# Batch 1's attention beside the first product, in eight and six units instead of ten and seven

## The chip, the cores and the metric

The kernel runs on one core of one Trainium2 chip. The time is device microseconds of one execution, as a median over several runs. A profiled execution shows every engine's instructions: PE (TensorE: matmuls, with the weight loads as PEld), DVE (VectorE), ACT (ScalarE), POOL (GpSimd) and SP (SyncE). PE's results go to PSUM, from where DVE or ACT bring them out.

## What is computed

Attention without a softmax for 8 batches, 12 heads, 448 positions and 64 columns a head, followed by one feed-forward layer with a residual:

```python
scores = scale * np.matmul(q, k.transpose(0, 1, 3, 2))
attn = np.maximum(scores, 0.0) ** 2 / S
attn_out = np.matmul(attn, v)
x = attn_out.transpose(0, 2, 1, 3).reshape(B, S, H * D)      # 768 columns
xn = (x - mean(x)) / np.sqrt(var(x) + 1e-06) * g_ln
out = x + np.maximum(xn @ w_ch1, 0.0) @ w_ch2                # 3072 columns between
```

The kernel takes and multiplies in bf16 and accumulates in fp32.

## The kernel before

**Tiles and stages.** A batch has three groups of four heads (`G = 3`; group n is batch n // 3). Its 448 positions are seven slots of 64 (`J = 7`). Attention is made per group: `scores` takes one or two slots of keys against a block of query positions, four 64x64 matmuls at a time in the four quarters of PE's array, into one PSUM tile `sc_ps`; ACT applies relu and writes `attn_sb` (L376), DVE squares it in place (L354, L380). `values` multiplies seven slots of a group with v in 28 such matmuls into a PSUM tile `av_ps`; DVE scales that into `xT_sb` (L403) and writes two more scaled chunks into `x_room` (`scaled`, L420). `centre` subtracts the mean over columns: ones times xT on PE, then six DVE operations.

The first product, `ffn1` (L672 on), takes one column of 128 of the 3072: six matmuls into a PSUM tile `h_ps`, then relu into `hT_sb`, by DVE (L690) or ACT (L692). `ffn1_head` (L708) does the first three columns in one go.

**The blocks.** Batches 0 and 1 are cut into two blocks of positions each, `BLK = (((0, 3), (3, 4)), ((0, 4), (4, 3)))` as (first slot, number of slots), so that the attention of one block runs beside `ffn1` of the block before. The order of the work is written out by hand; nothing reorders it, and every engine runs its part in the code's order. Two stretches matter here:

- The first: `ffn1` of batch 0's second block (256 positions a column), with four columns left over from its first block, beside the attention of batch 1's first block, which is 256 positions (41 to 66 us in the profile).
- The second: `ffn1` of batch 1's first block (256 positions) beside the attention of batch 1's second block, 192 positions (66 to 87 us).

`interleave` deals side units evenly among the main ones (`free` main units at the end are kept without any, `ahead` side units go first). The main units are the columns of `ffn1`; the side units come from `attention_block`: per group `unit(n, 0)` (slots 0 to 3, two score tiles) and `unit(n, 1)` (slots 4, 5 and 6, two score tiles, then the value product of the group before), in the first block with `transposed(n + 1)` between the two, then `last` (the last value product) and `centre`. In these two batches `transposed` has PE transpose q and k of a group into two PSUM tiles, which DVE copies out (L253); from batch 2 on (`by_dma`) it issues three transposing DMAs on SP instead, L312, L317 and L318.

**PSUM.** The pool `ps_sc` has three tiles of two banks (`[P, 2, 512]` fp32), which `scores`, `values`, `transposed`, `centre` and part of `ffn1_head` take in turn; `ps_mm` has two tiles of one bank, which the columns of `ffn1` take in turn.

**Who empties h_ps.** `since` counts columns since the last score visit: `scores` sets it to 0 and `values` to 9, `ffn1` adds one. While it is at most `turns`, DVE takes the column, else ACT. The squares of a block of batch 0 or 1 are not issued with their scores, but kept in `later` until `squares_now`, which every unit calls first, and `ffn1` at `since >= turns`:

```python
        since[0] += 1
        turns = 2 if (b, blk) == FIRST else 1
        if since[0] <= turns:
            nc.vector.tensor_scalar_max(hT[pair][:, ni, o:o + w], ps[:, :w], 0.0)
        else:
            nc.scalar.activation(hT[pair][:, ni, o:o + w], ps[:, :w], ACTF.Relu)
        if since[0] >= turns:
            squares_now()
```

After the two stretches come `ffn1` of batch 1's last block (87 to 99 us), the attention of batches 2 and 3 beside the second product of batches 0 and 1, and so on to the end. POOL's queue issues the loads: `load(n + 3, "v")` stands behind each value product of the second block and waits until that product has let go of its buffer.

Of the kernel before, what the change touches and what calls it, by code (L numbers as in the profile page):

```python
# [28 lines left out]
def kernel(  # L29
# [22 lines left out]
    nc = tc.nc  # L52
    P = 128
    HP = 64
    bf16 = mybir.dt.bfloat16
    fp32 = mybir.dt.float32
# [5 lines left out]
    J = S // HP  # L62
# [3 lines left out]
    K1 = d_model // P  # L66
    K2 = d_ff // P
    S2 = 2 * S
# [3 lines left out]
    score_scale = 1.0 / (D * S)  # L72
# [10 lines left out]
    xpool = ctx.enter_context(tc.tile_pool(name="x", bufs=1))  # L83
# [18 lines left out]
    x_room = wpool.tile([P, 2, K1, S + 2], bf16, tag="x_room", name="x_room")  # L102
# [44 lines left out]
    def load(n, names):  # L147
        if n >= len(groups):
            return
        b, m = groups[n]  # L150
        for name in names:
            if b == 1 and name != "v":
                o = (2 * m + "qk".index(name)) * 2 * S
                t = hold[:, o:o + 2 * S].rearrange("p (r s) -> p r s", r=2)
            elif name == "q":
                t = qbuf[m][:, D:D + 2 * S].rearrange("p (r s) -> p r s", r=2)
            else:
                t = slot(name, n)
            nc.gpsimd.dma_start(t, srcs[name][b][:, m:NP:G, :])  # L159
            qkv[name, b, m] = t  # L160
# [169 lines left out]

    FULL = (0, J)
    FIRST, LAST = (0, BLK[0][0]), (1, BLK[1][1])
    n_early = [0]

    def busy(n):
# [6 lines left out]
    def of(blk, b=0):  # L342
        o = b % 2 * S
        return slice(o + blk[0] * HP, o + sum(blk) * HP)
# [3 lines left out]
    def squares_now(n=None, but=0):  # L348

        if n is None or n in [k for k, _ in later]:
            for _, a in later[:len(later) - but]:
                nc.vector.tensor_mul(a, a, a)  # L354
            del later[:len(later) - but]

    def scores(n, slots, blk, act=False):
        g, w = st[groups[n]], blk[1] * HP
        ps = ps_sc.tile([P, 2, 512], fp32, tag="sc", name="sc_ps")
        for o, i in enumerate(slots):  # L360
            for r in range(2):
                rows = slice(r * HP, (r + 1) * HP)
                for hh in range(2):
                    cols = slice(hh * HP, (hh + 1) * HP)
                    nc.tensor.matmul(  # L365
                        ps[cols, r, o * w:(o + 1) * w], g["k"](i)[rows, cols],
                        g["q"](i, r)[rows, blk[0]:sum(blk), cols], start=True, stop=True)
        if groups[n][0]:
            a = apool.tile([P, 2, 512], bf16, tag="attn", name="attn_sb")
        else:  # L370
            o = n_early[0] % 12 * 1024
            a = early[:, o:o + 1024].rearrange("p (r s) -> p r s", r=2)
            n_early[0] += 1
        since[0] = 0
        a = a[:, :, :len(slots) * w]
        nc.scalar.activation(a, ps[:, :, :len(slots) * w], ACTF.Relu)  # L376
        if act:
            nc.scalar.activation(a, a, ACTF.Square)  # L378
        elif blk == FULL:
            nc.vector.tensor_mul(a, a, a)  # L380
        else:
            later.append((n, a))
        for o, i in enumerate(slots):
            g["attn"].append(a[:, :, o * w:(o + 1) * w])

    def values(n, blk):
        squares_now(n)
        b, m = groups[n]
        v_sb, g, w = qkv["v", b, m], st[groups[n]], blk[1] * HP
        ps = ps_sc.tile([P, 2, 512], fp32, tag="sc", name="av_ps")  # L390
        for j in range(J):
            for hh in range(2):
                rows = slice(hh * HP, (hh + 1) * HP)
                for pr in range(2):
                    cols = slice(pr * HP, (pr + 1) * HP)
                    i, r = g["where"](pr, j)
                    nc.tensor.matmul(  # L397
                        ps[cols, hh, :w], v_sb[rows, pr, j * D:(j + 1) * D],
                        g["attn"][i][rows, r, :], start=(j == 0), stop=(j == J - 1))
        if b // 2 not in xT:  # L400
            xT[b // 2] = xpool.tile([P, K1, S2], bf16, tag="xT", name="xT_sb")
        x = xT[b // 2][:, 2 * m:2 * m + 2, of(blk, b)]
        nc.vector.tensor_scalar_mul(x, ps[:, :, :w], score_scale)  # L403
        g["attn"] = []
        since[0] = 9
        if blk == FULL:
            return
        if b not in xc:
            xc[b] = x_room[:, b]
        if (b, blk) != FIRST:  # L410
            scaled(b, m, blk)

    def scaled(b, m, blk):

        for c in range(2 * m, 2 * m + 2):
            x, y = xT[b // 2][:, c, of(blk, b)], xc[b][:, c, of(blk)]
            if (b, blk) == FIRST:
                nc.scalar.mul(y, x, g_sb[:, c:c + 1])
            else:
                nc.vector.tensor_scalar_mul(y, x, g_sb[:, c:c + 1])  # L420

    def centre(b, blk):
        w = blk[1] * HP
        straight = (b, blk) == FIRST
        if straight:
            ps = ps_mm.tile([P, 512], fp32, tag="mm", name="sum_ps")[:, :w]
        else:
            ps = ps_sc.tile([P, 2, 512], fp32, tag="sc", name="sum_ps")[:, 0, :w]
        for c in range(K1):
            nc.tensor.matmul(  # L430
                ps, ones, xT[b // 2][:, c, of(blk, b)], start=(c == 0), stop=(c == K1 - 1))
        total = ps
        if not straight:
            total = room0[:, :7].rearrange("p c n -> p (c n)").bitcast(fp32)[:, :w]
            nc.scalar.copy(total, ps)
        for c in range(K1):
            nc.vector.scalar_tensor_tensor(
                xc[b][:, c, of(blk)], total, g_mean[:, c:c + 1], xc[b][:, c, of(blk)],
                op0=ALU.mult, op1=ALU.add)
# [63 lines left out]
    def transposed(n):  # L503

        if groups[n][0] < by_dma:
            transposes(*groups[n])
            return


        if by_dma * G < n < LATE:  # L510
            load(n + 2, "kq")
        keys_dma(n)
        queries_dma(n)
        if n == LATE + 1:
            put_off.append((n + 2, "kq"))
        elif n >= LATE:
            load(n + 2, "kq")

    def attention_block(b, blk):


        lo, hi, first = b * G, b * G + G, blk[0] == 0
        units = [lambda: transposed(lo)] if first else []

        def unit(n, part):
            squares_now()
            for i in range(4 * part, min(4 * part + 4, J), 2):
                scores(n, tuple(range(i, min(i + 2, J))), blk)
            if b == 1 and not first and part and n == hi - 1:
                transposed(hi)  # L530
            if part and n > lo:
                values(n - 1, blk)
                if not first:
                    load(n + 3, "v")
        for n in range(lo, hi):
            units.append(lambda n=n: unit(n, 0))
            if first and n + 1 < hi:
                units.append(lambda n=n: transposed(n + 1))
            units.append(lambda n=n: unit(n, 1))

        def last():
            values(hi - 1, blk)
            if b == 1 and not first:
                load(hi + 3, "v")
        units.append(last)
        units.append(lambda: centre(b, blk))
        return units
# [124 lines left out]
    def ffn1(b, ni, blk):  # L672


        pair, o, w = b // 2, b % 2 * S + blk[0] * HP, blk[1] * HP
        if pair not in hT:
            hT[pair] = hpool.tile([P, K2, S2], bf16, tag="hT", name="hT_sb")
        ps = ps_mm.tile([P, 512], fp32, tag="mm", name="h_ps")

        more, s = 2 if (b, blk) == LAST else 0, of(blk)  # L680
        for c in range(K1):
            nc.tensor.matmul(  # L682
                ps[:, :w + more], w1[:, c, ni * P:(ni + 1) * P], xc[b][:, c, s.start:s.stop + more],
                start=(c == 0), stop=(c == K1 - 1))
        if more:
            nc.vector.tensor_copy(fold["sums"][:, ni], ps[:, w:w + more])
        since[0] += 1
        turns = 2 if (b, blk) == FIRST else 1
        if since[0] <= turns:
            nc.vector.tensor_scalar_max(hT[pair][:, ni, o:o + w], ps[:, :w], 0.0)  # L690
        else:
# [3 lines that stand above are left out]
# [706 lines left out]
```

## Time and profile before

| | us |
|---|---|
| median of 3 runs | 514.32 |
| lowest and highest | 514.0, 515.42 |
| the profiled execution | 514.53 |
| its span, first to last instruction | 512.7 |

| busy in the span | us | share |
|---|---|---|
| PE | 504.5 | 98% |
| DVE | 387.3 | 76% |
| ACT | 309.4 | 60% |
| POOL | 129.6 | 25% |

The profile's views used here are: the chain of waits, which goes back from the last instruction to whatever released each; the busy time of each engine in a stretch; and the timeline, where instructions of one kind that follow one another stand in one row with the start of the first, the time from there to the end of the last, and their number. Matmuls are pipelined: each lasts about 0.27 us in a row while the next starts 0.11 us after it, so starts are to be compared, not ends.

### The profile page before, as it was taken

Reading aid. Unit: us, or ns where it says so; the run is one execution under the profiler, and the core shown is the slowest. Engines: PE = TensorE matmul, PEld = TensorE weight load, DVE = VectorE, ACT = ScalarE, POOL = GpSimd, SP = SyncE. Lnnn points to the kernel's source line nnn. Section 1 sums busy time; section 2 is a strip of 40 time slices with the busy share of each in tenths; the row PEclk is TensorE's granted clock in tenths of the full one; section 3 lists DMA queues with packets and bytes.
Section 4 is the critical chain, followed back from the end, with each engine's and each line's share of the span. In section 5 each row is a group of like instructions: output and inputs, shape, how many; then the busy total and the mean of one; then the engine's idle time right before and its main releaser. Section 6 shows DMA issues by size and latency. Waiting matters only on the chain.

```text
span 512.7 us, 11440 instructions
## 1 busy us (share of the span) xinstructions
PE 504.5 (98%) x4553; PEld 299.0 (58%) x4553; DVE 387.3 (76%) x745; ACT 309.4 (60%) x496; POOL 129.6 (25%) x182
## 2 busy tenths in 40 slices
PE   8899999999999999999999999999999999999996
PEld 6677788855555555555555555555555555556663
DVE  5775765389899888858789968858887968868663
ACT  5966676488678266657757266639979366630000
POOL 8335112012301266321201099501100022200000
PEclk9999999999999999999999999999999999999999
DMA  9999999999969985329995989304997393322222
GB/s 196 206 207 206 211 206 159 158 145 185 190 141 166 185 197 175 130 65 168 187 245 106 186 186 184 94 11 84 188 185 173 71 215 124 94 77 63 63 61 61
DMA packets 124486, 76.31 MB, mean 149 GB/s; under 512 B 80562, under 2 KB 120498, under 8 KB 124434
## 3 DMA queue, kind: packets, MB, share of 16 engines
q1 hardware_dynamic: 93730, 41.38, 39.6%
q0 software_dynamic: 28544, 30.91, 38.3%
q10 hardware_dynamic: 2160, 3.31, 2.8%
q8 instruction: 35, 0.57, 0.5%
q14 instruction: 17, 0.14, 0.1%
HBM read 64.69 MB, written 17.89 MB: 161 GB/s over the span
## 4 chain that ended last, share of the span: by engine, by line
PE 94%; ACT 2%; DVE 1%; DMA 1%; issue 1%; SPq 0%; DVEq 0%
PE m_ps L899 28%; PE o_ps L741 20%; PE o_ps L1109 9%; PE m_ps L1109 8%; PE h_ps L682 8%; PE sc_ps L365 8%; PE av_ps L397 6%; PE h_ps L726 2%; PE h_ps L708 2%; PE o_ps L1071 2%; ACT early L376 1%; PE tr_ps L250 1%; DMA stage_sb<-in_q_dram 1%; DMA out_dram<-o_room 1%; DVE o_room L1125 0%
## 5 line engine op out<-in xcount | busy, mean ns | idle before, releaser
L376 ACT ACTIVATE attn_sb<-sc_ps 128x896 bf16<-128x896 f32 (+4 forms) x150 | 126.3, 902 | 39.4 <-PE sc_ps L365 34.5
L903 ACT ACTIVATE hT_sb<-m_ps 128x448 bf16<-128x448 f32 x144 | 78.2, 543 | 52.0 <-PE m_ps L899 49.3
L741 PE MATMUL o_ps<-w,hT_sb 128*128 128x384 bf16 x624 | 108.3, 327 | 0.0
L741 PEld LDWEIGHTS <-hT_sb 128*128 128x128 bf16 x624 | 58.2, 98 | 45.7 <-issue 10.1
L380 DVE TENSOR_TENSOR attn_sb<-attn_sb 128x896 bf16<-128x896 bf16 x98 | 61.7, 645 | 19.8 <-ACT attn_sb L376 19.1
L682 PE MATMUL h_ps<-x_room,w 128*128 128x256 bf16 (+2 forms) x384 | 43.8, 263 | 0.4 <-ACT early L376 0.3
L1109 PEld LDWEIGHTS <-hT_sb 128*128 128x128 bf16 x312 | 29.7, 98 | 22.1 <-issue 3.0
L980 DVE TENSOR_TENSOR m_ps<-x_room,m_ps 128x448 f32<-128x448 f32 x36 | 22.6, 629 | 23.8 <-ACT hT_sb L903 23.6
L682 PEld LDWEIGHTS <-w 128*128 128x128 bf16 x384 | 33.8, 97 | 7.2 <-issue 2.8
L899 PEld LDWEIGHTS <-w 128*128 128x128 bf16 x246 | 23.9, 97 | 23.1 <-issue 0.4
L1109 PEld LDWEIGHTS <-x_room 128*128 128x128 bf16 x252 | 24.2, 98 | 17.4 <-issue 1.6
L403 DVE TENSOR_SCALAR xT_sb<-av_ps 128x896 bf16<-128x896 f32 (+2 forms) x30 | 27.0, 901 | 9.3 <-PE av_ps L397 9.2
L964 ACT COPY x_room<-m_ps 128x448 f32<-128x448 f32 x36 | 19.1, 531 | 21.6 <-PE m_ps L899 20.7
L899 PEld LDWEIGHTS <-w_sum 128*128 128x128 bf16 x210 | 20.5, 98 | 19.1
L159 POOL DMA_DIRECT2D k_sb<-in_k_dram x15 | 10.7, 712 | 81.1 <-DMA kT_sb<-k_sb 57.3
L899 PE MATMUL m_ps<-x_sum,w 128*128 128x448 bf16 x120 | 29.1, 352 | 0.1
L659 DVE BATCH_NORM_STATS2 stats<-xtok_sb 128x6 f32<-128x384 bf16 x56 | 28.3, 548 | 0.0
L159 POOL DMA_DIRECT2D v_sb<-in_v_dram x20 | 14.2, 711 | 55.5 <-PE sc_ps L365 40.7
L365 PE MATMUL sc_ps<-qT_sb,kT_sb 64*64 64x448 bf16 x392 | 28.2, 358 | 0.0
L692 ACT ACTIVATE hT_sb<-h_ps 128x256 bf16<-128x256 f32 (+1 forms) x49 | 18.0, 368 | 16.1 <-PE h_ps L682 15.2
L378 ACT ACTIVATE attn_sb<-attn_sb 128x896 bf16<-128x896 bf16 x28 | 26.6, 950 | 0.9
L397 PE MATMUL av_ps<-attn_sb,v_sb 64*64 64x448 bf16 (+2 forms) x532 | 26.2, 331 | 0.1
(196 smaller groups left out, 871.7 us busy)
## 6 DMA issues: line engine op xcount, KB each, us to landing
out_dram<-o_room SPq DMA_DIRECT2D x108, 96.0 KB, 2.8
w<-in_moe_w_ch_dram POOLq DMA_DIRECT2D x12, 384.0 KB, 14.3
w<-in_moe_w_ch_dram POOLq DMA_DIRECT2D x4, 1152.0 KB, 20.0
q_sb<-in_q_dram POOLq DMA_DIRECT2D x20, 224.0 KB, 6.2
v_sb<-in_v_dram POOLq DMA_DIRECT2D x20, 224.0 KB, 6.6
k_sb<-in_k_dram POOLq DMA_DIRECT2D x15, 224.0 KB, 6.0
kept<-room SPq DMA_DIRECT2D x4, 480.0 KB, 2.6
kept<-w_sum SPq DMA_DIRECT2D x16, 96.0 KB, 1.7
```

What stands on the lines that cost most here:

```text
L365: nc.tensor.matmul(ps[cols, r, o * w:(o + 1) * w], g["k"](i)[rows, cols], g["q"](i, r)[rows, blk[0]:sum(blk), cols], start=True, stop=True)
L376: nc.scalar.activation(a, ps[:, :, :len(slots) * w], ACTF.Relu)
L378: nc.scalar.activation(a, a, ACTF.Square)
L380: nc.vector.tensor_mul(a, a, a)
L397: nc.tensor.matmul(ps[cols, hh, :w], v_sb[rows, pr, j * D:(j + 1) * D], g["attn"][i][rows, r, :], start=(j == 0), stop=(j == J - 1))
L403: nc.vector.tensor_scalar_mul(x, ps[:, :, :w], score_scale)
L659: nc.vector.bn_stats(stats[:, n], xtok[pair][:, n * G:(n + 1) * G, t, :])
L682: nc.tensor.matmul(ps[:, :w + more], w1[:, c, ni * P:(ni + 1) * P], xc[b][:, c, s.start:s.stop + more], start=(c == 0), stop=(c == K1 - 1))
L741: nc.tensor.matmul(ps[:, :DH], hT[pair][:, ki, t * P:(t + 1) * P], w2[:, ki, cols], start=(o == 0), stop=(o == K2 - 1))
L899: nc.tensor.matmul(ps, *at, start=(first and c == 0), stop=(c == KQ - 1), skip_group_check=not first)
L903: nc.scalar.activation(hT[pair][:, n + KH * row, half * S:(half + 1) * S], ps, ACTF.Relu)
L1109: nc.tensor.matmul(ps, x[:, ki], y[ki] if isinstance(y, list) else y[:, ki], start=(first and ki == 0), stop=(ki == KH - 1), skip_group_ch ...
```

## The change

`attention_block` builds batch 1's units by hand. Units are now bundles of `two` (two slots' scores), `one` (the seventh slot's scores, and with them the value product of the group before), and `transposed`. The first block is `transposed`, then per group three `two`s and a bundle of `one`, with the next group's transposes ahead of it: eight units and `centre`. The second is six and `centre`, some with slots of two groups. Inside `one` the value product takes the columns of the `sc_ps` tile that the seventh slot leaves free, its matmuls are issued between the slot's scores and its relu, and the scaling behind that relu. `values` is split for it. Last, `turns` is 3 in the two stretches, and `since` is 0 after a shared value product, where it was 9.

```diff
+    BESIDE = [(0, BLK[0][1]), (1, BLK[1][0])]
...
-    def scores(n, slots, blk, act=False):
+    def scores(n, slots, blk, act=False, then=None):
         g, w = st[groups[n]], blk[1] * HP
         ps = ps_sc.tile([P, 2, 512], fp32, tag="sc", name="sc_ps")
...
+        end = then(ps[:, :, w:]) if then else None
         if groups[n][0]:
             a = apool.tile([P, 2, 512], bf16, tag="attn", name="attn_sb")
...
-    def values(n, blk):
+        if end:
+            end()
+            since[0] = 0
+
+    def values(n, blk, ps=None):
+        if ps is None:
+            values_of(n, blk, ps_sc.tile([P, 2, 512], fp32, tag="sc", name="av_ps"))()
+        else:
+            return values_of(n, blk, ps)
+
+    def values_of(n, blk, ps):
         squares_now(n)
...
-        ps = ps_sc.tile([P, 2, 512], fp32, tag="sc", name="av_ps")
...
+        def out_of():
...
+            nc.vector.tensor_scalar_mul(x, ps[:, :, :w], score_scale)
+            g["attn"] = []
+            since[0] = 9
...
+            if (b, blk) != FIRST:
+                scaled(b, m, blk)
+        return out_of
...
-            if b == 1 and not first and part and n == hi - 1:
-                transposed(hi)
...
+        def last():
+            values(hi - 1, blk)
+            if b == 1 and not first:
+                load(hi + 3, "v")
+
+        def two(n, i):
+            scores(n, (i, i + 1), blk)
+
+        def one(n):
+            scores(n, (J - 1,), blk, then=(lambda ps: values(n - 1, blk, ps)) if n > lo else None)
+            if n > lo and not first:
+                load(n + 3, "v")
+
+        def bundle(*parts):
+            def run():
+                squares_now()
+                for f, *at in parts:
+                    f(*at)
+            return run
+        if b == 1:
+            n = lo
+            if first:
+                units += [bundle((two, n, 0), (two, n, 2), (two, n, 4)),
+                          bundle((transposed, n + 1), (one, n)),
+                          bundle((two, n + 1, 0), (two, n + 1, 2), (two, n + 1, 4)),
+                          bundle((transposed, n + 2), (one, n + 1)),
+                          bundle((two, n + 2, 0), (two, n + 2, 2), (two, n + 2, 4)),
+                          bundle((one, n + 2))]
+            else:
+                units += [bundle((two, n, 0), (two, n, 2)),
+                          bundle((two, n, 4), (one, n), (two, n + 1, 0)),
+                          bundle((two, n + 1, 2), (two, n + 1, 4), (one, n + 1)),
+                          bundle((two, n + 2, 0), (two, n + 2, 2), (two, n + 2, 4)),
+                          bundle((transposed, hi), (one, n + 2))]
+            return units + [last, lambda: centre(b, blk)]
...
-        turns = 2 if (b, blk) == FIRST else 1
+        turns = 2 if (b, blk) == FIRST else 3 if (b, blk) in BESIDE else 1
```

More of the change, by code (lines that the diff above doesn't have):

```diff
@@ L399, in values @@
                         g["attn"][i][rows, r, :], start=(j == 0), stop=(j == J - 1))
[L400 to L411, printed above, removed]
+        def out_of():
+            if b // 2 not in xT:
+                xT[b // 2] = xpool.tile([P, K1, S2], bf16, tag="xT", name="xT_sb")
+            x = xT[b // 2][:, 2 * m:2 * m + 2, of(blk, b)]
+            nc.vector.tensor_scalar_mul(x, ps[:, :, :w], score_scale)
+            g["attn"] = []
+            since[0] = 9
+            if blk == FULL:
+                return
+            if b not in xc:
+                xc[b] = x_room[:, b]
+            if (b, blk) != FIRST:
+                scaled(b, m, blk)
+        return out_of
     def scaled(b, m, blk):
@@ L539, in attention_block @@
             units.append(lambda n=n: unit(n, 1))
[L541 to L544, printed above, removed]
         units.append(last)
```

## The prediction

> **What bounds the kernel now.** I read the page's chain of waits first, then the busy time by stretch for the two blocks that the diff touches, then the timelines of PE and DVE in them, then one row of ACT. The chain:
>
> ```profile
> PE 94%; ACT 2%; DVE 1%; DMA 1%; issue 1%; SPq 0%; DVEq 0%
> ```
>
> The end is set by PE, so a microsecond that PE loses or saves where it never waits moves the end by a microsecond. The two blocks, by stretch (length, PE, PEld, DVE, ACT, POOL busy):
>
> ```profile
> 41.00:65.80 24.80, 24.80 (x397) 19.61 (x396) 16.30 (x34) 17.25 (x33) 7.74 (x11) 1.00 1.18 209
> 66.00:87.20 21.20, 21.20 (x318) 17.14 (x318) 12.51 (x36) 15.29 (x32) 3.39 (x5) 1.00 1.24 172
> ```
>
> PE is busy all of both, and the view of waits has none of PE's from 40 to 100 us. DVE is 66% and 59% busy. PE's timeline (start, length) shows what a change of shape costs:
>
> ```profile
> 11.06 0.58 PE L250 MATMUL tr_ps<-identity,q_sb 128*64 128x128 bf16 x14
> ...
> 11.96 0.44 PE L365 MATMUL sc_ps<-early 64*64 64x192 bf16 x12
> ...
> 51.15 0.97 PE L250 MATMUL tr_ps<-identity,xtok_sb 128*64 128x128 bf16 x28
> 52.06 1.49 PE L682 MATMUL h_ps<-x_room,w 128*128 128x256 bf16 x12
> 53.47 0.52 PE L365 MATMUL sc_ps<-xtok_sb 64*64 64x256 bf16 x12
> 53.83 0.93 PE L397 MATMUL av_ps<-attn_sb,spare 64*64 64x256 bf16 x28
> 54.69 1.48 PE L682 MATMUL h_ps<-x_room,w 128*128 128x256 bf16 x12
> 56.10 0.63 PE L365 MATMUL sc_ps<-xtok_sb 64*64 64x256 bf16 x16
> 56.67 1.48 PE L682 MATMUL h_ps<-x_room,w 128*128 128x256 bf16 x12
> ```
>
> Unbroken, 18 such h_ps matmuls (63.98 us, 2.13 long, 0.27 one) start 0.109 apart; I call six a column. Four 64*64 score matmuls run at once, 0.109 a set. From 52.06 to 53.47 are 1.41 us, 12 steps and 0.09 more; from 56.10 to 56.67 are 0.57, four sets and 0.13 more. So a visit to the scores costs 0.22 us of changes. A transposes' visit costs the same: 0.09 in, and 28 steps of 0.028 and 0.12 out.
>
> DVE's timeline, first of the first block, then of the second:
>
> ```profile
> 50.61 0.42 DVE L690 TENSOR_SCALAR hT_sb<-h_ps 128x256 bf16<-128x256 f32 x1 [0.62 <-PE h_ps L682]
> 50.95 1.36 DVE L354 TENSOR_TENSOR attn_sb<-attn_sb 128x1024 bf16<-128x1024 bf16 x2
> 52.22 1.15 DVE L253 COPY xtok_sb<-tr_ps 128x896 bf16<-128x896 bf16 x2
> 54.81 0.69 DVE L403 TENSOR_SCALAR xT_sb<-av_ps 128x512 bf16<-128x512 f32 x1 [1.44 <-PE av_ps L397]
> 55.54 0.48 DVE L420 TENSOR_SCALAR x_room<-xT_sb,g_sb 128x256 bf16<-128x256 bf16 x2
> 55.93 1.02 DVE L354 TENSOR_TENSOR attn_sb<-attn_sb 128x1024 bf16<-128x1024 bf16 x2
> ...
> 75.96 0.56 DVE L403 TENSOR_SCALAR xT_sb<-av_ps 128x384 bf16<-128x384 f32 x1 [0.94 <-PE av_ps L397]
> 76.55 0.45 DVE L420 TENSOR_SCALAR x_room<-xT_sb,g_sb 128x192 bf16<-128x192 bf16 x2
> 76.92 0.82 DVE L354 TENSOR_TENSOR attn_sb<-attn_sb 128x768 bf16<-128x768 bf16 x2
> ```
>
> DVE starts things in the code's order. From start to start an eviction takes 0.34 (0.42 until it has ended), a pair of wide squares 1.27, so three 1.91, two transposes' copies 1.15, a product's scaling with its two followers 1.12. In the second block they are 0.5 a square of 768 (mean 551 ns, overlapping), 0.28 one of 384, 0.96 the scaling.
>
> **The change, part by part.** *Fewer visits.* In the first block two transposes' visits go in with the score visit behind them. From 11.06 to 11.96 transposes hand over to scores in 0.90, as they do to h_ps in 0.91, so each join saves 0.09 in and about 0.01: 0.2 for two. In the second block one score visit fewer saves 0.22 us. Together 0.42 us on the path. Matmul and weight load counts stay.
>
> *The shared tile.* It saves one of three ps_sc turns a group, worth nothing now, as PE waits for none. It adds an order: the slot's relu comes after the 28 value matmuls in the code, the scaling after that relu. How the program treats two engines in one bank is seen where columns of one h_ps tile are read by DVE (L712) and others by ACT:
>
> ```profile
> 89.05 0.33 ACT L715 ACTIVATE hT_sb<-h_ps 128x192 bf16<-128x192 f32 x1 [1.14 <-DVE x_room L712]
> ```
>
> ACT waited although its columns are others. So I let relu wait for the product, scaling for relu. The Trainium skill (PSUM — Partial Sum Buffer, "PSUM bank collisions raise a hardware error") asks that engines be kept apart by bank and not by address; a reader who took the free columns for free to use at once would by that rule be wrong. With the wait a 256-wide relu (605 ns mean) lies ahead of the scaling; without it the scaling starts at the product's end. This decides something in one product of four (below, about 0.5 us); elsewhere DVE is later anyway.
>
> *The evictions.* Now the first h_ps column after a score visit goes to DVE, the rest to ACT (`since`), and after a value product all go to ACT. After the change three columns go to DVE after every score visit, after a shared product too (`since[0] = 0` behind `end`), and the squares wait for the third or the next bundle. There are only two ps_mm tiles, so **the third column after a visit cannot start before the first one's eviction has ended**, and that stands in DVE's queue behind everything of the bundle.
>
> Take "columns u1, u2, then transposes, one slot and a value product, then u3, u4, u5" of the first block. From u2's last matmul start, DVE: 0.27 to its end and 0.04 to its eviction; eviction 0.34, three squares 1.91, two copies 1.15, scaling 1.12, u3's eviction 0.42, 0.05 to PE: 5.30 us. PE up to u5: 0.20 and 0.90 for the transposes, 1.00 for one slot and the product (53.47 to 54.69 less two sets), 12 steps 1.31: 3.41. **Stall 1.89.** Without a product (the first group): DVE 4.18, PE 0.20 + 0.90 + 0.24 + 1.31 = 2.65: **1.53**; this contains a wait of 0.26 for the third relu, as three of 1.0 follow one another on ACT. Without transposes (third group): DVE 4.15, PE 0.20 + 1.00 + 1.31 = 2.51: **1.64**. First block: 5.06.
>
> Second block, group 3's product: its squares start only behind the third column's eviction, at 0.31 + 0.34, so its last attention slot is ready after 1.45 + 0.06; PE would be there at 0.20 + 0.42 (five sets) + 0.44: **0.45**. Then relu of the slot (0.94 from the product's last start, ACT being full), scaling 0.96, eviction 0.42 and latencies 0.13 are 2.45 against PE's 0.20 + 1.31, rounded 1.53: **0.92**. The three slots of group 5: squares 1.28 ahead of the next eviction, 2.40 against 2.14: **0.25**. Group 4's product: 0.31 + 0.34 + three squares 1.5 + 0.96 + 0.42 + 0.05 = 3.58 against 0.20 + 0.78 + 1.31 = 2.29: **1.29**. The closing product waits for a square that moved behind the third eviction: **0.36**. Second block: 3.27.
>
> *Moved issues.* The transposed group 6 issues three transposing DMAs on SP, now ahead of group 5's last scores. SP already ran them at 72.71, 74.17 and 77.24, ahead of that place, as their data arrives: nothing. POOL's v loads keep their place behind products; they feed groups 7 to 9, whose first product starts at 124.8 us, and land 6.6 us after issue: nothing while some 40 us lie between. The attention buffers (nine) hold at most eight live tiles: no new wait. ACT loses about as many evictions as DVE gains and stays below PE.
>
> **Sum:** 5.06 + 3.27 - 0.42, and -0.12 for a wait of group 4's product on a square that goes (58.08 to 58.56 is 0.48, against 0.36 at 53.47) = **+7.8 us**. After 87 us PE waits for nothing that the block could have absorbed: from there on the chain is PE but for about 4 us of short ACT, DVE and DMA pieces, whose producers shift with it. The profiled run took 514.53 (span 512.7), 0.2 above the median 514.32. So 522.2.
>
> Bounds for what no row shows: a DVE queue without gaps could run closer; their DVE parts add up to some 21 us, so pieces 10% shorter take 2.1 off and pieces 5% longer add 1.0.
>
> **Rivals.**
> 1. *Not slower: DVE keeps out of the way.* If the third column never waits for DVE (a third bank, or evictions that overtake), only the 0.42 and 0.12 are left: 513.8, within 0.3%. For it: DVE was idle for a third of the block. Against: DVE's order follows the code in all rows, and 5.30 against 3.41 leaves room for 1.9 us of error. It decides from a DVE sum under 3.4 us. Chance 0.08.
> 2. *Half of it.* The second block's sums are under 1.3 each and lean on the relu's wait; if its pieces overlap as DVE's spare 41% would allow, only the first block's 5.06 - 0.54 stays: 518.8. Chance 0.12.
> 3. *A slower clock as well.* The granted clock is 1.00 up to 510.67 us, through PE gaps of up to 0.67 us at the start; gaps of 1.9 are not shown. If each of five long stalls cost a further 1 us at half clock: 527.2. The Trainium skill (TensorE: Matmul & The Clock Gate, part 1) puts the drop at an idle window of some 3.4 us; by that rule none of my stalls would bring it. Chance 0.06.
>
> **How the numbers follow.** The forecast, 522.2, has 0.74, with a range of its own of 519.5 to 524.5. The range for 8 in 10 reaches over rival 2: 517.5 to 525.5. About 0.3% (1.5 us) can be told from no change: faster by more needs a mechanism I don't see, 0.03; within, 0.07; slower 0.90.
>
> **What would show it.** PE's timeline: after the bundles with the single slot, gaps of 0.9 to 1.9 us in front of the third h_ps column, released by DVE's hT_sb evictions (now L690), five times; DVE without idle from a visit's second column to the next visit; DVE evictions of h_ps in the two stretches up from 8 to 30; 14 visits of other shapes instead of 17. The L708 groups at 66.5 and 87.3 come later by about 4.7 and 7.8. Wrong if those gaps are under 0.5 us, or if they are there but a later stretch shrinks.

## The result, and the profile after

| | before | after |
|---|---|---|
| median, us | 514.16 (6 runs) | 521.7 (6 runs) |
| lowest and highest, us | 513.82, 515.42 | 521.21, 525.56 |
| ratio of the times, 95% interval | | 1.0151 (1.0132 to 1.017) |
| profiled execution, us | 514.53, span 512.7 | 525.56, span 523.8 |
| first to second three-column group, us | 28.86 | 33.12 |
| second to third, us | 20.83 | 23.59 |
| both: the stretch that the change touches | 49.69 | 56.71 |

The three-column groups are those of `ffn1_head` (L708 before, L749 after) with which batch 0's second block, batch 1's first and batch 1's second begin: at 37.63, 66.49 and 87.32 us before, at 40.69, 73.80 and 97.39 after. I use this stretch as the measure below, since it leaves out what differs from execution to execution elsewhere.

The kernel is 7.5 us slower. The profiled execution of after is the slowest of its six, and its span is 11.1 us longer, which is more than the change: 3.05 us of that lie ahead of the first three-column group, where nothing was edited; 7.02 lie in the stretch; 0.94 come at 317 to 320 us of before's clock, where DVE's statistics waited for a transposing DMA that landed 6.42 us after its issue; in before PE waits for nothing there. A later arrival does not bring that wait by itself: e2 below reaches the place 6.5 us later than before and loses nothing there. Between these places the matmuls of the two executions run at a constant distance, to within 0.1 us.

The first 3.05 us are seen in the chain of waits (start, length). These transposes are the same instructions in both. Before:

```profile
8.61 0.27 PE busy_ps L340 x3
8.89 0.92 PE tr_ps L250 x28
```

After:

```profile
9.85 0.43 PE busy_ps L341 x3
10.28 1.65 PE tr_ps L250 x28
```

Matmuls ran at about half speed until 17.3 us in this execution, until 5.5 us in that of before; these are the times of the trace's first record of the full clock. The view by stretch gives a granted clock of 1.00 from 0 to 12 us in both; the slow start is seen in the matmuls' lengths, not there.

The page's chain after, and PE's waits from 40 to 108 us (us in total, times, longest), a view that was empty before:

```profile
PE 89%; DVE 5%; ACT 2%; DMA 2%; issue 1%; SPq 0%; DVEq 0%; ACTq 0%
```

```profile
PE h_ps L723 <- DVE hT_sb L731: 5.2, 5, 1.4
PE sc_ps L366 <- ACT attn_sb L378: 0.4, 2, 0.2
PE av_ps L407 <- DVE attn_sb L355: 0.2, 1, 0.2
```

Five waits of a column for a column's eviction by DVE (the view counts from the end of the matmul before, so it gives less than the gaps between starts used below). The two blocks by stretch (length, PE, PEld, DVE, ACT, POOL busy) are no longer full on PE; DVE has gained 3.95 and 4.1 us of work, ACT has lost 3.6 and 3.9:

```profile
44.07:73.35 29.28, 25.32 (x398) 20.02 (x398) 20.25 (x46) 13.61 (x21) 4.97 (x8) 1.00 1.18 209
73.35:97.28 23.93, 21.89 (x318) 17.48 (x318) 16.61 (x47) 11.39 (x21) 3.50 (x5) 1.00 0.63 96
```

PE's timeline in the first block, from the second column after a bundle of scores to the next bundle:

```profile
54.31 1.48 PE L723 MATMUL h_ps<-x_room,w 128*128 128x256 bf16 x12
55.73 0.97 PE L250 MATMUL tr_ps<-identity,xtok_sb 128*64 128x128 bf16 x28
56.90 0.30 PE L366 MATMUL sc_ps<-xtok_sb 64*64 64x256 bf16 x4 [0.20 <-ACT attn_sb L378]
57.01 0.96 PE L407 MATMUL sc_ps<-attn_sb,spare 64*64 64x256 bf16 x28
57.90 1.49 PE L723 MATMUL h_ps<-x_room,w 128*128 128x256 bf16 x12
60.63 0.82 PE L723 MATMUL h_ps<-x_room,w 128*128 128x256 bf16 x6 [1.24 <-DVE hT_sb L731]
```

and DVE's in the same time:

```profile
55.84 0.43 DVE L731 TENSOR_SCALAR hT_sb<-h_ps 128x256 bf16<-128x256 f32 x1 [0.23 <-PE h_ps L723]
56.18 1.89 DVE L355 TENSOR_TENSOR attn_sb<-attn_sb 128x1024 bf16<-128x1024 bf16 x3
57.98 1.15 DVE L253 COPY xtok_sb<-tr_ps 128x896 bf16<-128x896 bf16 x2
59.04 0.68 DVE L414 TENSOR_SCALAR xT_sb<-sc_ps 128x512 bf16<-128x512 f32 x1
59.76 0.48 DVE L432 TENSOR_SCALAR x_room<-xT_sb,g_sb 128x256 bf16<-128x256 bf16 x2
60.16 0.75 DVE L731 TENSOR_SCALAR hT_sb<-h_ps 128x256 bf16<-128x256 f32 x2
```

The first column behind the bundle was computed by 58.7 (57.90, five starts of 0.109, 0.27 for the last). Its eviction starts at 60.16, after three squares, two copies, the scaling and its two followers, with no idle time in between; it ends at 60.58, and the third column starts 0.05 later. The single slot's relu, on ACT, begins after the value matmuls of its tile:

```profile
58.02 0.60 ACT L378 ACTIVATE attn_sb<-sc_ps 128x512 bf16<-128x512 f32 x1 [1.17 <-PE sc_ps L407]
```

In the first block DVE's own queue is later than that relu. In one product of the second block it is not, and there DVE waits for the relu:

```profile
82.83 0.56 DVE L414 TENSOR_SCALAR xT_sb<-sc_ps 128x384 bf16<-128x384 f32 x1 [0.60 <-ACT attn_sb L378]
```

### The profile page after: what moved, and what is told of

Read it like the earlier page. It is cut to its first block, busy times and chain, and to the rows that moved or that the text cites. A ratio compares the mean times of both kernels' runs of the same rounds, so it can differ in the third digit from the quotient of the medians.

```text
span 523.8 us, 11439 instructions
## 1 busy us (share of the span) xinstructions
PE 509.9 (97%) x4553; PEld 302.8 (58%) x4553; DVE 395.5 (76%) x767; ACT 302.1 (58%) x474; POOL 129.8 (25%) x182
## 4 chain that ended last, share of the span: by engine, by line
PE 89%; DVE 5%; ACT 2%; DMA 2%; issue 1%; SPq 0%; DVEq 0%; ACTq 0%
PE m_ps L940 25%; PE o_ps L782 19%; PE o_ps L1150 9%; PE m_ps L1150 8%; PE sc_ps L366 7%; PE h_ps L723 6%; PE av_ps L407 5%; PE h_ps L767 2%; PE h_ps L749 2%; PE o_ps L1112 2%; ACT early L378 1%; DVE attn_sb L355 1%; DMA xtok_sb<-xT_sb 1%; PE tr_ps L250 1%; DVE hT_sb L731 1%
## 5 line engine op out<-in xcount | busy, mean ns | idle before, releaser
L782 PE MATMUL o_ps<-w,hT_sb 128*128 128x384 bf16 x624 | 108.2, 326 | 0.0
L1150 PEld LDWEIGHTS <-x_room 128*128 128x128 bf16 x252 | 24.3, 98 | 17.3 <-issue 1.6
L414 DVE TENSOR_SCALAR xT_sb<-av_ps 128x896 bf16<-128x896 f32 (+2 forms) x26 | 24.5, 943 | 5.3 <-PE av_ps L407 5.0
L1150 PE MATMUL o_ps<-w,hT_sb 128*128 128x384 bf16 x144 | 25.9, 327 | 0.0
L494 DVE SCALAR_TENSOR_TENSOR w<-w,g_sb,x_room 128x512 bf16<-128x512 bf16 x36 | 25.7, 737 | 0.0
```

Source lines behind the costliest of these rows:

```text
L494: nc.vector.scalar_tensor_tensor(w, w, g_sb[:, c:c + 1], fold["means"][i % 2].rearrange("p (h n) -> p h n", h=2), op0=ALU.mult, op1=ALU.add)
L782: nc.tensor.matmul(ps[:, :DH], hT[pair][:, ki, t * P:(t + 1) * P], w2[:, ki, cols], start=(o == 0), stop=(o == K2 - 1))
L1150: nc.tensor.matmul(ps, x[:, ki], y[ki] if isinstance(y, list) else y[:, ki], start=(first and ki == 0), stop=(ki == KH - 1), skip_group_ch ...
```

## The experiments

Three theories. **Q**, the queue: the third column after a visit waits for the first one's eviction, which stands in DVE's queue behind the bundle's work, as predicted. **S**, the shared tile: the relu and the scaling that follow one another behind a product cost the time. **V**, the visits: fewer and larger visits crowd ACT and DVE, whoever empties the columns. The stretch (first to third three-column group) and the times:

| | stretch, us | median, us | ratio to before, 95% |
|---|---|---|---|
| before | 49.69 | 514.16 | |
| after | 56.71 | 521.7 | 1.0151 (1.0132 to 1.017) |
| e1, ACT empties after a shared product | 51.06 | 515.56 | 1.0033 (1.0005 to 1.0061) |
| e2, products in tiles of their own | 56.46 | 521.16 | 1.0142 (1.0111 to 1.0173) |
| e3, the evictions alone, in the old units | 51.97 | 517.56 | 1.0056 (1.0029 to 1.0083) |
| e4, units and shared tile, old evictions | 49.67 | 514.84 | 1.0019 (0.9994 to 1.0044) |
| e5, e4 with products in tiles of their own | 51.37 | 516.33 | 1.0034 (1.0014 to 1.0053) |
| e6, after without batch 1's squares | 53.78 | 518.46 | 1.0076 (1.0046 to 1.0106) |
| e7, three to DVE after scores only | 50.00 | 515.16 | 1.0004 (0.9988 to 1.0021) |
| e8, e4 with one relu of three on DVE | 49.07 | 514.43 | 1.0000 (0.9981 to 1.0020) |
| e9, e6 with products in tiles of their own | 51.81 | 516.35 (1 run) | |
| e10, e8 again | 49.07 | 514.16 | 0.9988 (0.9973 to 1.0002) |

The medians of before that came with e1 to e4, e5 to e8 and e9 to e10 were 514.15, 514.27 and 514.40.

**One line undone.** In `scores`:

```diff
         if end:
             end()
-            since[0] = 0
```

> The change with one line undone: after a shared value product the next columns go to ACT again, not to DVE. Measure: from the start of the three-column group of batch 0's second block to that of batch 1's last block, 49.69 us before and 56.71 after the change. Theory Q (the third column waits for the first one's eviction, which stands in DVE's queue behind squares, copies and scaling): the four gaps of 1.40, 1.52, 0.91 and 1.16 us behind shared products go, the gap of 1.05 behind the first single slot, which has no product, stays, and small waits: 51.2 us, the time near 515.7. Rival S (the shared tile: relu waits for the product, the scaling for relu): nothing changes there, 56.7 and 521.7. Rival V (fewer and larger visits crowd relu and squares whoever empties the columns): over 55.

Measured: 51.06 and 515.56. Of PE's five waits on DVE's evictions one is left, behind the single slot that has no product (whose `since` is still 0):

```profile
PE h_ps L722 <- DVE hT_sb L730: 0.9, 1, 0.9
PE sc_ps L366 <- ACT attn_sb L378: 0.4, 2, 0.2
```

The visits are the change's, so V falls as the main cause, and 5.65 of 7.02 us hang on who empties three columns after a product. The relu still waits for the product in this kernel, so that wait alone does not cost the time; but the run also takes away the evictions that a chain of product, relu and scaling would hold up. Whether that chain or the queue held them is for the next run.

**The shared tile undone.**

```diff
-            scores(n, (J - 1,), blk, then=(lambda ps: values(n - 1, blk, ps)) if n > lo else None)
+            scores(n, (J - 1,), blk)
+            if n > lo:
+                values(n - 1, blk)
+                since[0] = 0
```

> The change, but each value product has an ps_sc tile of its own again; three columns still go to DVE after every visit. Theory Q: DVE's queue is as long, so the gaps stay or move in front of the product, whose tile is now held by a transposes' copy in the same queue: 56.7 to 57.5 us between the three-column groups, the time 521.5 to 522.5. Rival S: the gaps of 1.40, 1.52, 0.91 and 1.16 shrink by the relu's 0.6 each or go: 49.7 to 54.5. Rival V: no change, 56.7.

Measured: 56.46 and 521.16, a little under what Q gave. Waits changed places, their sum nearly stayed: four on evictions, and two of the product (L407) that were not there, on a relu of ACT and not, as expected, on DVE's copies:

```profile
PE h_ps L726 <- DVE hT_sb L734: 3.5, 4, 1.2
PE av_ps L407 <- ACT attn_sb L378: 1.4, 2, 0.7
```

So S falls as the main cause: it gave 54.5 at most. With its order taken away, DVE's queue and the product's waits for its tile cost nearly the same time.

**The evictions alone**, in the units of before:

```diff
+    BESIDE = [(0, BLK[0][1]), (1, BLK[1][0])]
...
                 values(n - 1, blk)
+                if b == 1:
+                    since[0] = 0
...
-        turns = 2 if (b, blk) == FIRST else 1
+        turns = 2 if (b, blk) == FIRST else 3 if (b, blk) in BESIDE else 1
```

> The kernel before with the change's evictions alone: its ten and seven units and own tiles stay, but three columns go to DVE after every score visit and every value product of batch 1 but the last of a block. Theory Q: gaps come here too where the third column follows, smaller, since a unit has two squares and not three: 49.7 + 3.1 = 52.8 us, the time near 517.3. Rivals S and V: 49.7 to 50.2, the time near 514.3.

Measured: 51.97, 2.28 over before and not 3.1. The evictions cost by themselves, but mostly in another way than a column's wait: the closing products wait for squares that have moved behind the third eviction.

```profile
PE av_ps L398 <- DVE attn_sb L355: 1.3, 2, 0.8
PE h_ps L685 <- DVE hT_sb L693: 0.4, 1, 0.4
```

The median is 3.4 us over before, the stretch 2.28; the profiled execution also lost 1.2 us between 292 and 320 us, in late waits at 317 to 320 us, as in after, and at 292 us.

**Units and shared tile without the evictions.** Against after:

```diff
         if end:
             end()
-            since[0] = 0
...
             scores(n, (J - 1,), blk, then=(lambda ps: values(n - 1, blk, ps)) if n > lo else None)
+            since[0] = 9
...
-        turns = 2 if (b, blk) == FIRST else 3 if (b, blk) in BESIDE else 1
+        turns = 2 if (b, blk) == FIRST else 1
```

> The change's units and shared tile with the evictions of before: one column to DVE after a score visit, none after the bundle with the single slot. Theory Q: no gap in front of a third column; two waits of some 0.27 for the third relu and 0.2 in the second block against 0.42 saved: 49.4 to 50.2 us between the three-column groups, the time 513.9 to 514.7. Rival S: four products at 0.5 each stay, 51.3 to 52. Rival V: over 55.

Measured: 49.67, as before, and no wait on an eviction. So the 7.02 us are the evictions in the new units; the new units without them neither cost nor save. What eats their saving is in the timeline:

```profile
43.98 2.86 ACT L378 ACTIVATE attn_sb<-sc_ps 128x1024 bf16<-128x1024 f32 x3
...
46.89 0.30 PE L366 MATMUL sc_ps<-qT_sb 64*64 64x256 bf16 x4 [0.20 <-ACT attn_sb L378]
```

Three relus in a row end at 46.84, and the single slot, whose tile the third of them empties, starts 0.05 later. It comes 0.42 after the last transpose, against 0.15 where nothing is waited for: 0.27, twice. In the second block a third column loses another 0.20.

**Own tiles in e4**, with the edit of e2 less its last line.

> The change's units with the evictions of before, and each value product in a tile of its own. What the shared tile is worth by itself: the units with the shared tile took 49.67 us between the three-column groups. If sharing is only an order (relu waits for the product) and no gain, 49.5 to 49.7. If the new units need the turn that it saves (three score tiles, two transposes and the single slot go round three tiles before the product, so the product waits until DVE has copied the transposes out of its tile, behind three squares): one wait of some 1.1 us in the first block and 0.8 in the second, 51.4 to 51.7, the time near 516.

Measured: 51.37, at the lower edge of the second case. Sharing is worth 1.70 us in the new units. The size is what was expected, the place is not: the product does not wait for DVE's copies but for a relu.

```profile
52.90 0.60 ACT L378 ACTIVATE attn_sb<-sc_ps 128x512 bf16<-128x512 f32 x1
53.14 1.15 DVE L253 COPY xtok_sb<-tr_ps 128x896 bf16<-128x896 bf16 x2
...
53.55 0.96 PE L406 MATMUL av_ps<-attn_sb,spare 64*64 64x256 bf16 x28 [0.69 <-ACT attn_sb L378]
```

It starts 0.05 after that relu and before either copy has ended, so the copies do not hold its tile. Why this relu does was not settled.

**Without squares.**

```diff
-            for _, a in later[:len(later) - but]:
-                nc.vector.tensor_mul(a, a, a)
+            for k, a in later[:len(later) - but]:
+                if groups[k][0] == 0:
+                    nc.vector.tensor_mul(a, a, a)
```

> The change with the squares of batch 1's attention left out (the output is not the reference's). Three squares take 1.8 us of DVE's queue. If squares in the queue were all of it, no gap: 49.3 to 49.7 us. Theory Q with the shared tile's order: the gap of 1.05 behind the slot without a product goes, but behind a product relu 0.63, scaling 1.12 and the eviction 0.42 still follow one another after its end, 2.3 us against the 1.25 that PE has to the third column: gaps of about 1.0 in the first block (two) and 0.7 to 1.4 in the second (two), 53.2 to 53.8 us, the time near 518.

Measured: 53.78. The gap behind the slot without a product is gone, the four behind products stay, at 0.8 to 1.4 us. DVE, with no squares to do, is idle there:

```profile
54.01 0.69 DVE L415 TENSOR_SCALAR xT_sb<-sc_ps 128x512 bf16<-128x512 f32 x1 [1.14 <-ACT attn_sb L379]
54.74 0.48 DVE L433 TENSOR_SCALAR x_room<-xT_sb,g_sb 128x256 bf16<-128x256 bf16 x2
55.14 0.75 DVE L732 TENSOR_SCALAR hT_sb<-h_ps 128x256 bf16<-128x256 f32 x2
```

It waits for the relu, which waits for the product. So the shared tile's order is a second chain of nearly the same length under the squares: where one is taken away, the other holds the column.

**Without squares, in own tiles**: the edits of e6 and e2 together.

> Squares of batch 1 left out as before (the output is not the reference's), and each value product in a tile of its own, so that the scaling need not wait for the single slot's relu. With the shared tile and no squares it was 53.78 us between the three-column groups. If the relu between product and scaling is what the shared tile costs there: the four gaps behind products shrink by the relu's 0.63 (0.47 in the second block) and more, and a wait of the product for its tile of up to 0.8 comes in: 51.5 to 52.3 us. If the engines of one tile don't wait for one another: 53.8 again.

Measured: 51.81. The first block's two gaps behind products fall from 1.02 and 1.08 to 0.39 each, by the relu's 0.63. In the same place DVE starts 0.6 us earlier, counted from the first three-column group (37.08 in e6, 37.18 here), released by the product itself:

```profile
53.51 0.69 DVE L415 TENSOR_SCALAR xT_sb<-av_ps 128x512 bf16<-128x512 f32 x1 [0.53 <-PE av_ps L408]
```

**Three columns to DVE after scores only**: e4 with the change's `turns` of 3 left in.

> The change with DVE taking three columns only behind the bundles of scores; behind the bundle with the single slot, with or without a product, ACT takes them. Theory Q: no gap in front of a third column; the two waits for the third relu and 0.3 of a product in the second block that waits for its squares, which stand behind the third eviction: 49.9 to 50.3 us, the time near 514.6. If three evictions on DVE cost wherever they stand: over 51.

Measured: 50.00, no wait on an eviction. DVE may take three columns where its queue is empty, behind a bundle of scores; it does not gain anything there either, since one product waits 0.28 for its squares.

**A version meant to beat both.** In e4 ACT's three relus in a row are what is left, and DVE is idle when they start. The first of three goes to DVE:

```diff
-        nc.scalar.activation(a, ps[:, :, :len(slots) * w], ACTF.Relu)
+        if dve:
+            nc.vector.tensor_scalar_max(a, ps[:, :, :len(slots) * w], 0.0)
+        else:
+            nc.scalar.activation(a, ps[:, :, :len(slots) * w], ACTF.Relu)
```

with `dve` set for the first `two` of each bundle of three score tiles, and for the one at the head of the bundle with group 4's single slot in the second block.

> The change's units and shared tile, the evictions of before, and the first of three score tiles of a bundle gets its relu from DVE, which is idle there, so ACT has two in a row and not three. If the 0.42 us of fewer visits is eaten by the two waits for the third relu (0.27 each) and by 0.2 in the second block where ACT's chain of three relus holds a column: 48.8 to 49.2 us between the three-column groups against 49.69 before, the time some 0.6 below that of before. If those waits are something else: 49.6 or more.

> The kernel with the first of three relus on DVE once more. Its stretch took 49.07 us, 0.62 below that of before, but its profiled execution lost 0.8 us at 177 and 320 us to landings of DMAs that an execution of before did not wait for. If that was chance: 49.07 again, the rest 425.4, a median of 513.6 to 513.8. If an earlier end of the stretch brings those waits: 49.07, the rest 426 or more, a median of 514.1 to 514.4.

Measured: 49.07 both times, 0.62 under before, and PE's view of waits is empty again in the two blocks; the two waits of 0.27 are gone, so they were the third relu. ACT now has the bundle's relus done 2.62 us after its first score matmul (43.28), in e4 it was 3.32 (43.52 to 46.84):

```profile
43.74 1.23 DVE L379 TENSOR_SCALAR attn_sb<-sc_ps 128x1024 bf16<-128x1024 f32 x1 [1.43 <-PE sc_ps L366]
43.96 1.94 ACT L381 ACTIVATE attn_sb<-sc_ps 128x1024 bf16<-128x1024 f32 x2 [0.19 <-PE sc_ps L366]
```

The whole time doesn't show it: 514.43 beside 514.27, then 514.16 beside 514.40, and both intervals include no change. The 0.6 expected of the time did not come, and neither case set down for the second run did: its rest lies between the two. That rest, the span after the stretch, took 426.45 and 425.78 against 425.42: 0.16 of that comes at 177 us in both executions, 0.63 at 320 us in the first alone, at the same late DMA as in the profiled execution of after, and the remainder in small steps. Whether the 0.16 is the price of arriving earlier was not tried.

## Why the prediction was right

**The place and the releaser** were right: five waits of a third column on a DVE eviction; 30 evictions by DVE in the two blocks, as counted; 14 visits.

**The third column behind a product with transposes**, 1.89: the gap is 1.40 more than a step, and 0.27 went ahead of it at the single slot's scores, 1.67 together. From u2's last matmul start to u5, DVE's sum of 5.30 took 5.10 (55.53 to 60.63). The difference is in pieces that run closer in a full queue: three squares 1.80 for 1.91, two copies 1.07 for 1.15. The 1.15 was also misread: it is the length of the pair to its end, not from start to start as the prediction says; the two copies start 0.53 apart before the change too. The prediction's bounds named a queue that runs closer; the stalls went that way, about half as far as its lower bound of 2.1.

**The others**, predicted and measured: without a product 1.53 and 1.05 + 0.27; without transposes 1.64 and 1.52; in the second block 0.45 and 0.28, 0.92 and 0.91, 0.25 and 0.17, 1.29 and 1.16, 0.36 and 0.33. Sum 8.33 and 7.36. The stretch grew by 7.02 where the sum said 7.8: the stalls came out 0.97 smaller, and the saving of 0.54 that I took off came out 0.2 smaller, 0.13 of it in uneven steps behind the wait of group 3's product and the rest in steps of a few hundredths. The three-column groups came later by 4.26 and 7.02 us, where the prediction gave 4.7 and 7.8.

**The time** was nearer than the sum: 522.2 predicted (514.32 and 7.8 are 522.1), 521.7 measured. Part of that is luck. The median grew by 7.54 us, 0.5 more than the stretch, and where the other 0.5 lies is not known, since only one execution of after was traced.

**The wait of relu for product and of scaling for relu** was taken from one row (L715), and holds: 1.17 us of ACT idle ahead of the relu at 58.02. Its price was put at about 0.5 in one product of four, "elsewhere DVE is later anyway". The first part is seen in the row at 82.83, where DVE waits 0.60 for the relu, and the gap was right (0.91 for 0.92). The second is seen in DVE's rows, which have no idle time ahead of the scaling at 59.04; e6 and e9 show how near it was: without the squares the relu's 0.63 is on the path in the first block too.

**The shared tile as worth nothing** was wrong as a general remark. PE waited for no ps_sc tile before; in the new units it would, and sharing saves 1.70 us there (e5 against e4). In the change itself, where DVE's queue holds everything up, its loss and its gain nearly cancel (e2: 0.25).

**The saving of fewer visits** could not show in the change, but it is there: e8's stretch is 0.62 shorter than that of before. That is the 0.42 for visits and 0.34 of two products' waits for squares (0.12 and 0.22) that its earlier squares end, less some 0.16 that a column still loses in the second block.

**Rivals.** The first needed a DVE sum under 3.4 us; it was 5.10. The second, half of it, took the second block's sums for doubtful; they came to 2.85 of 3.27. The third, a lower clock, did not come: the matmuls behind each of the five gaps start 0.109 apart as ever. By the Trainium skill's idle window of some 3.4 us (TensorE: Matmul & The Clock Gate, part 1) gaps of 1.5 should leave the clock alone, and the 0.109 in the trace agrees.

**After the stretch** nothing absorbed it, as predicted: matmul for matmul the distance stays at 10.07 to 10.11 us up to the late DMA at 317 us.

## What to carry to other kernels

With two PSUM tiles in turn, the engine that empties the first decides when the third starts, as in the five gaps here (a third tile was not tried): look at what stands ahead of that eviction in its queue, not at how busy the engine is on average (DVE was at 66% before this change). A second product put into a tile's free columns frees a tile and makes its readers follow one another; add their lengths to the chain from the product to the next eviction. And when units are made larger, count how many results of one visit one engine has to empty before the next visit can have a tile.

## What the runs showed of the hardware that was not expected

- Full clock came at 17.3 us in one execution and at 5.5 us in another of the same first instructions; it cost 3.05 us of time, more than most of the differences studied here. A stretch of the trace between two fixed instructions compared kernels to within some hundredths where the times scattered by one to four microseconds.
- Operations of DVE that follow one another without a gap start closer than they last: squares of 128x1024 lasted 0.68 us and started 0.60 apart, copies out of PSUM lasted 0.62 and started 0.53 apart.
- Three to four places after the stretch (177, 292, 317 to 320 us) lose 0.2 to 1.3 us in some executions and nothing in others, where DVE's statistics (at 320 in after, e3 and e8) or an output buffer (at 177 in e7, at 292 in e3) wait for a DMA. Six of the executions traced (e1, e2, e4, e5, e6, e9) lose nothing at any of them.
